# Lone-exponential step of the attention stage: VectorE copies one transposed half out of PSUM, minimum and reciprocals stand later

## Chip, cores and metric

The kernel runs on one core of one Trainium2 chip. The metric is the device time of one execution in microseconds (us). TensorE is PE (its weight loads PEld), VectorE is DVE, ScalarE is ACT, GpSimd is POOL, and the SyncE queue is SP.

## What is computed

Bucketed attention over 4 batches, 8 heads, 768 positions and head dimension 64, followed by a mixture of 8 experts in which each token goes to one expert. Cut to what matters:

```python
mask = q_bucket[:, :, :, None] == k_bucket[:, :, None, :]       # 6 sign bits of q @ proj, k @ proj
scores = scale * np.matmul(q, k.transpose(0, 1, 3, 2))          # (4, 8, 768, 768)
scores = np.where(mask, scores, -1e9)
attn = np.exp(scores - scores.max(-1, keepdims=True))
attn = attn / (attn.sum(-1, keepdims=True) + 1e-9)
x = np.matmul(attn, v)                                          # then reshaped to (3072, 512)
e = argmax(x @ w_gate); y = relu(x @ w1[e]) @ w2[e]             # times two gates
```

## The kernel before

The attention stage works in 192 steps (`NSTEP`), each for one tile of 128 queries by 768 keys of one head. Six steps make a period (`PER`), so there are 32 periods; a pair of heads takes two of them. In the text the periods are numbered 0 to 31 and the steps of a period 0 to 5 (`k` in the code), and "the first step" is step 0, "the fourth step" is step 3, which the change touches.

Per tile, in this order:

- `scores` (L536): PE makes the tile in PSUM with four matmuls, into one of two buffers `ps_s`. VectorE reads it once (L540), writes it negated and masked to SBUF as `sc`, and has the row minimum `mn` of it as an accumulated output. This frees the `ps_s` buffer, so the scores of step s need the minimum of step s-2.
- `soft` (L548): ScalarE takes the exponential in place, with the row sum as accumulated output. One exponential stands alone in each period: that of step 1's tile, issued at the end of step 2. The other five are issued in the next period's step 0.
- `normal` (L555, L556, L558): for two tiles at a time, VectorE adds 1e-9 to the sums and takes reciprocals, and GpSimd multiplies both tiles. For the pair with the lone exponential this stands in step 3.
- `transposed` (L569, L574, L572): six steps after its scores, PE transposes the tile, three 128x128 blocks into one `ps_t` buffer (there are two) and three into the other; each half is copied to `pts` in SBUF, by ScalarE (L574), and for the last six tiles the second half by VectorE (L572). The transposes of step s need the copies of step s-1 to be done, half by half.
- `weighted` (L584): in step 0 PE multiplies the transposed tiles with the values, and VectorE copies the result out (L587).

All four compute engines run in the order in which the program is written (`manual_schedule`); the loop at the end of the attention stage writes it. Other work is hung into it by `plan` (behind the step's transposes) and `block` (at named places of step 0). What matters here:

- In step 0 of every even period from 2 to 28, the next pair of heads is prepared: GpSimd makes two high parts `xl` (`split_hi`, L494) ahead of step 0's exponentials, and VectorE makes four low parts `yl` (`split_lo`, L502) between its reciprocals; the first low part of a head needs that head's high part. GpSimd runs its multiplications of the period before ahead of `split_hi`.
- `tokens` (L628, three transposes on PE and a reduction on VectorE) stands in step 2 of periods 9, 10, 17, 18, 25, 26 and 31.
- `ranks` (L695 to L700, five small operations of VectorE) stands in step 2 of periods 11, 19 and 27; `pick` (L784 to L793, seven) in step 2 of period 28; `table` (six matmuls on PE) in step 3 of periods 13, 21 and 29; `early_turn` (four transposes on PE, a cast by ScalarE, and a subtraction by VectorE, L272) in steps 2 and 4 of period 30.
- GpSimd's small tables of constants stand in periods 3 to 6.

So of the 30 periods 2 to 31, thirteen have none of this in steps 2 and 3 and none of it just before (2 to 8, 14 to 16, 22 to 24); the text calls them plain. Periods 12 and 20 stand behind the periods with ranks.

Of the kernel before, what the change touches and what calls it, by code (L numbers as in the profile page):

```python
# [14 lines left out]
ALU = mybir.AluOpType  # L15
# [8 lines left out]
HS = S // 2  # L24
# [21 lines left out]
PER = 6  # L46
NFB = F // P
MASKED = 1.0e9
# [11 lines left out]
def lsh_attention_then_moe(  # L60
# [10 lines left out]
    nc = tc.nc  # L71
# [16 lines left out]
    def signed():  # L88

        for h, s in ((0, 1.0), (1, -1.0)):  # L90
            hs = slice(h * D, (h + 1) * D)
            c = 2 * NB * h
            nc.gpsimd.tensor_scalar(pjc[hs, c:c + NB], pj[hs, 0:NB], s, 0.0, ALU.mult, ALU.add)
            nc.gpsimd.tensor_scalar(pjc[hs, c + NB:c + 2 * NB], pj[hs, 0:NB], -s, 0.0, ALU.mult, ALU.add)
# [276 lines left out]
    with ExitStack() as actx:  # L371
# [6 lines left out]
        NSTEP = 12 * NP  # L378
# [7 lines left out]
        LAG = PER  # L386
# [91 lines left out]
        def first_low(part):  # L478

            st = pairs[0]  # L480
            xl, yl, xr, qk = st["xl"][1], st["yl"][1], st["xr"][1], st["qk"][1]
            if part == 0:
                nc.vector.tensor_tensor(xr[D:P], qk[D:P], f32(xl[D:P]), ALU.subtract)
                nc.gpsimd.tensor_scalar(xl[D:P], qk[0:D], -0.125, 0.0, ALU.mult, ALU.add)  # L484
            else:
                nc.vector.scalar_tensor_tensor(yl[0:D], qk[0:D], -0.125, f32(xl[0:D]), ALU.mult, ALU.subtract)
# [35 lines left out]
        def tile_of(s):  # L522

            g, hf, i = s // 12, (s % 12) // 6, s % 6
            t, j = (i % 3, i // 3) if s // 6 in (0, 2) else (i // 2, i % 2)
            return g, hf, 3 * hf + t, j

        def scores(s):
            g, hf, t, j = tile_of(s)
            st = pairs[g]  # L530
            qs = slice(t * P, (t + 1) * P)
            ss = ps_s.tile([P, 2, 512], F32, name="ps_s")
            kb = D + 2 * NB
            for l, r, k, first in ((st["xl"][j], st["xr"][j], P, True), (st["yl"][j], st["yr"][j], kb, False)):
                for n in range(2):
                    nc.tensor.matmul(ss[:, n, 0:HS], l[0:k, qs], r[0:k, n * HS:(n + 1) * HS],  # L536
                                     start=first, stop=not first)
            sc = tp.tile([P, 2, HS], F32, name="sc", bufs=LAG + 2)
            mn = sp.tile([P, 1], F32, name="mn", bufs=PER + 2)
            nc.vector.tensor_scalar(sc, ss[:, :, 0:HS], MASKED, None, ALU.min, ALU.min, accum_out=mn)  # L540
            return sc, mn

        def soft(s, sc, mn):
            if s % GROUP == 0:
# [12 lines left out]
            for k in range(GROUP):  # L557
                nc.gpsimd.tensor_scalar(live[s0 + k], live[s0 + k], rs[:, k:k + 1], 0.0, ALU.mult, ALU.add)  # L558

        def transposed(s, pr):  # L560
            g, hf, t, j = tile_of(s)
            hb, t = s // 6, t - 3 * hf
            if s % 6 == 0:
                blocks[hb] = [tp.tile([P, NT, HS], F32, name=f"pts{n}") for n in range(2)]
            pts = blocks[hb][j]
            for h in range(2):
                tr = ps_t.tile([P, 3, P], F32, name="ps_t")
                for c in range(3):
                    nc.tensor.transpose(tr[:, c], pr[:, (3 * h + c) * P:(3 * h + c + 1) * P], ident)  # L569
                dst = pts[:, 3 * h:3 * h + 3, t * P:(t + 1) * P]  # L570
                if h and s >= NSTEP - PER:
                    nc.vector.tensor_copy(dst, tr)  # L572
                else:
                    nc.scalar.copy(dst, tr)  # L574
# [286 lines left out]
        with tc.manual_schedule(engines=MANUAL):  # L861
# [7 lines left out]
            def turn_idle(n):  # L869
                for i in range(n):  # L870
                    nc.tensor.transpose(idle[:, i % 3], ident, ident)
# [4 lines left out]
            live = {}  # L876
# [12 lines left out]
            def normals():  # L889
                while ready:  # L890
                    normal(ready.pop(0))
# [5 lines left out]
            for s in range(NSTEP + LAG):  # L897
                k = s % PER
                if s < NSTEP:
                    live[s] = scores(s)  # L900
                    raw.append(s)
                if s < 2:
                    first_low(s)
                if s == 1:
                    signed()
                if 0 < s < 3:
                    turn_idle(6)
                if s < PER:
                    normals()
                    softs(1)  # L910
                elif k == 0:
                    now("head")
                    softs(2)
                    now("early")
                    normals()
                    now("amid")
                    softs(2)
                    normals()
                    for when in ("logits", "matmuls", "behind"):
                        now(when)  # L920
                    softs(1)
                elif k == 3:
                    normals()
                if s >= LAG:
                    transposed(s - LAG, live.pop(s - LAG))
                if s >= PER and k == 2:
                    softs(1)
                for fn in at.get(s, ()):
                    fn()
# [257 lines left out]
```

## Time and profile before

| | |
|---|---|
| median of 3 runs | 764.87 us (764.33 to 765.95) |
| profiled execution | 763.37 us, of which the trace's span is 761.6 us |
| PE busy | 744.8 us, 98% of the span |
| DVE busy | 489.1 us, 64% |
| ACT busy | 458.8 us, 60% |
| POOL busy | 378.4 us, 50% |

The attention stage takes about 444 us of the span, up to the first of the experts' products at 443.94 us. A matmul's end is modelled in this profile, so a busy PE can still be waiting: one reads PE from the start of one row to the start of the next. The same six transposes and four matmuls follow each other in every step, so a step that starts late beside its neighbours shows a wait, even where the view lists no idle time.

### The profile page before, as it was taken

To read this page: it belongs to the slowest core of one execution; us is meant where nothing else is said; L and a number is where in the kernel's file an instruction comes from. 1 tells how busy PE (TensorE), PEld (TensorE's weight loads), DVE (VectorE), ACT (ScalarE), POOL (GpSimd) and SP (SyncE) were. 2 spreads that over 40 slices of the span, in tenths; PEclk is the share of its full clock that TensorE was granted. 3 is DMA by queue.
4 is the path that set the end of the run, shared out by engine and by line. 5 is a ranking of instruction groups with operands and counts; after the bars stand their busy time and mean duration, and the time that the engine had idled before them with its cause. 6 is when DMAs were issued, how large, how long until landed. Compare 5 with 4: busy or idle time off the path is not lost. (4 is left out here: it accounts for less than half of the span.)

```text
span 761.6 us, 13702 instructions
## 1 busy us (share of the span) xinstructions
PE 744.8 (98%) x4690; PEld 606.9 (80%) x4690; DVE 489.1 (64%) x1042; ACT 458.8 (60%) x928; POOL 378.4 (50%) x418
## 2 busy tenths in 40 slices
PE   7799999999999999999999999999999999999996
PEld 5677777768777686767778678988999999989895
DVE  5767766888776798767898775346354546465540
ACT  5688887887887787787787822343333434443331
POOL 7456645544554555455456932645446364645201
PEclk9999999999999999999999999999999999999999
DMA  4565555646455556645455332463445454537501
GB/s 168 135 138 124 131 138 130 125 111 133 110 135 127 128 111 136 141 106 124 82 114 131 79 96 76 150 236 107 133 137 159 153 159 146 184 127 234 187 12 40
DMA packets 84799, 98.89 MB, mean 130 GB/s; under 512 B 57999, under 2 KB 59439, under 8 KB 84720
## 3 DMA queue, kind: packets, MB, share of 16 engines
q1 hardware_dynamic: 79376, 84.58, 43.0%
q0 software_dynamic: 5200, 13.31, 5.5%
q8 instruction: 40, 0.66, 0.4%
q14 instruction: 39, 0.32, 0.1%
q10 hardware_dynamic: 144, 0.02, 0.0%
HBM read 59.49 MB, written 13.11 MB: 95 GB/s over the span
## 5 line engine op out<-in xcount | busy, mean ns | idle before, releaser
L558 POOL TENSOR_SCALAR sc<-sc,rsum 128x768 f32<-128x768 f32 x192 | 185.8, 982 | 191.2 <-DVE rsum L556 101.3
L540 DVE TENSOR_SCALAR_CACHE_REDUCE sc<-ps_s 128x768 f32<-128x768 f32 x192 | 182.7, 955 | 56.3 <-PE ps_s L536 53.4
L574 ACT COPY pts<-ps_t 128x384 f32<-128x384 f32 x378 | 162.8, 483 | 83.8 <-PE ps_t L569 82.8
L548 ACT ACTIVATE sc<-sc,mn 128x768 f32<-128x768 f32 x192 | 178.2, 935 | 7.7 <-DVE sc L540 7.7
L569 PE MATMUL ps_t<-ident,sc 128*128 128x128 f32 x1152 | 161.0, 276 | 3.2 <-POOL sc L558 2.3
L569 PEld LDWEIGHTS ps_t<-ident,sc 128*128 128x128 f32 x1152 | 133.6, 141 | 33.1 <-POOL sc L558 15.8
L584 PE MATMUL ps_a<-pts,vt 128*64 128x384 f32 x768 | 131.1, 490 | 0.0
L536 PE MATMUL ps_s<-xr,xl 128*128 128x384 f32 x384 | 115.3, 381 | 4.4 <-POOL xl L484 2.2
L584 PEld LDWEIGHTS ps_a<-pts,vt 128*64 128x64 f32 x768 | 52.2, 137 | 67.7 <-issue 67.5
L326 DVE SCALAR_TENSOR_TENSOR hl<-ps_s,hh 128x256 fp32r<-128x256 f32 (+8 forms) x40 | 34.0, 849 | 107.8 <-ACT hh L325 107.8
L536 PE MATMUL ps_s<-yr,yl 76*128 76x384 f32 x384 | 99.7, 341 | 0.7 <-POOL yr L446 0.5
L315 PE MATMUL ps_s<-xh,w1h 128*128 128x256 f32 (+7 forms) x288 | 96.9, 336 | 0.0
L315 PE MATMUL ps_s<-xlo,w1h 128*128 128x256 f32 (+7 forms) x288 | 95.3, 331 | 0.0
L315 PE MATMUL ps_s<-xh,w1l 128*128 128x256 f32 (+7 forms) x288 | 95.1, 330 | 0.0
L289 POOL DMA_INDIRECT xq<-x_dram,idx x75 | 82.7, 1103 | 23.7 <-issue 20.8
L332 POOL DMA_INDIRECT out_dram<-yo,sid x29 | 30.8, 1062 | 115.4 <-ACT yo L331 57.0
L325 ACT ACTIVATE hh<-ps_s 128x256 fp32r<-128x256 f32 (+8 forms) x40 | 29.0, 726 | 96.0 <-PE ps_s L315 96.0
L536 PEld LDWEIGHTS ps_s<-yr,yl 76*128 76x128 f32 x384 | 70.6, 191 | 1.2 <-POOL yr L446 1.2
L536 PEld LDWEIGHTS ps_s<-xr,xl 128*128 128x128 f32 x384 | 58.5, 192 | 8.0 <-DVE sc L540 3.8
L315 PEld LDWEIGHTS ps_s<-xh,w1h 128*128 128x128 f32 x288 | 54.1, 188 | 2.0 <-issue 0.6
L315 PEld LDWEIGHTS ps_s<-xlo,w1h 128*128 128x128 f32 x288 | 54.1, 188 | 1.3 <-DVE xlo L272 0.2
L315 PEld LDWEIGHTS ps_s<-xh,w1l 128*128 128x128 f32 x288 | 54.1, 188 | 1.1
(206 smaller groups left out, 1014.3 us busy)
## 6 DMA issues: line engine op xcount, KB each, us to landing
w_raw<-in_w_dram SPq DMA_DIRECT2D x34, 512.0 KB
qk<-in_qkT_dram SPq DMA_DIRECT2D x32, 384.0 KB
xh<-in_w_dram SPq DMA_DIRECT2D x14, 512.0 KB
xlo<-in_w_dram SPq DMA_DIRECT2D x14, 512.0 KB
vt<-in_v_dram SPq DMA_DIRECT2D x16, 384.0 KB
xr<-xl SPq DMA_DIRECT2D x30, 192.0 KB
yr<-xl SPq DMA_DIRECT2D x30, 192.0 KB
xr<-yl SPq DMA_DIRECT2D x30, 192.0 KB
```

The lines of the kernel that those rows point to most:

```text
L289: nc.gpsimd.indirect_dma_start(out=xq[:, k * P:(k + 1) * P], out_offset=None, in_=x_dram.rearrange("n (a f) -> (n a) f", a=NB32), in_offse ...
L315: nc.tensor.matmul(ps, l, r, start=first and k == 0, stop=last and k == len(pairs) - 1)
L325: nc.scalar.activation(hh, ph, AF.Relu)
L326: return lambda: nc.vector.scalar_tensor_tensor(hl, ph, 0.0, f32(hh), ALU.max, ALU.subtract)
L332: nc.gpsimd.indirect_dma_start(out=out[:, :], out_offset=bass.IndirectOffsetOnAxis(ap=sid[0:n, r, a:a + 1], axis=0), in_=yo[0:n], in_offse ...
L536: nc.tensor.matmul(ss[:, n, 0:HS], l[0:k, qs], r[0:k, n * HS:(n + 1) * HS], start=first, stop=not first)
L540: nc.vector.tensor_scalar(sc, ss[:, :, 0:HS], MASKED, None, ALU.min, ALU.min, accum_out=mn)
L548: nc.scalar.activation(pr, pr, AF.Exp, bias=mn, scale=-1.0, accum_out=sums[s // GROUP][:, k:k + 1])
L558: nc.gpsimd.tensor_scalar(live[s0 + k], live[s0 + k], rs[:, k:k + 1], 0.0, ALU.mult, ALU.add)
L569: nc.tensor.transpose(tr[:, c], pr[:, (3 * h + c) * P:(3 * h + c + 1) * P], ident)
L574: nc.scalar.copy(dst, tr)
L584: nc.tensor.matmul(st["av"][j * D:(j + 1) * D], st["v"][:, j, c], blocks[hb][j][:, c], start=(c == 0), stop=(c == NT - 1))
```

## The change

In periods 2 to 31, in step 3 alone:

- VectorE, not ScalarE, copies the first half of the transposed tile out of PSUM (L572 in place of L574); ScalarE keeps the second half.
- That step's minimum (L540) is issued behind this copy, no longer right behind the step's matmuls.
- The addition and reciprocal for the pair with the lone exponential, and GpSimd's two multiplications that need them, are issued in step 4, behind that step's minimum, no longer in step 3.

```diff
@@ scores @@
-            nc.vector.tensor_scalar(sc, ss[:, :, 0:HS], MASKED, None, ALU.min, ALU.min, accum_out=mn)
-            return sc, mn
+            return (sc, mn), lambda: nc.vector.tensor_scalar(sc, ss[:, :, 0:HS], MASKED, None, ALU.min, ALU.min,
+                                                             accum_out=mn)
@@ transposed @@
-        def transposed(s, pr):
+        def transposed(s, pr, behind=False):
...
-                if h and s >= NSTEP - PER:
+                if h and s >= NSTEP - PER or behind and not h:
                     nc.vector.tensor_copy(dst, tr)
                 else:
                     nc.scalar.copy(dst, tr)
@@ the loop over steps @@
-                    live[s] = scores(s)
+                    live[s], least = scores(s)
                     raw.append(s)
+                    if s < 2 * PER or k != 3:
+                        least()
...
-                elif k == 3:
+                elif k == 4 or k == 3 and s < 2 * PER:
                     normals()
                 if s >= LAG:
-                    transposed(s - LAG, live.pop(s - LAG))
+                    transposed(s - LAG, live.pop(s - LAG), 2 * PER <= s < NSTEP and k == 3)
+                    if 2 * PER <= s < NSTEP and k == 3:
+                        least()
```

VectorE's order in a plain period before, from the last work of step 0 on. The first three minimums are those of steps 1 to 3, the next three those of steps 4, 5 and 0:

```order
L596 STREAM_TRANSPOSE xb<-ot 128x384
L540 TENSOR_SCALAR sc,mn<-ps_s 128x768 x3
L555 TENSOR_SCALAR rsum<-rsum 128x2
L556 RECIPROCAL rsum<-rsum 128x2
L540 TENSOR_SCALAR sc,mn<-ps_s 128x768 x3
L502 SCALAR_TENSOR_TENSOR yl<-qk,pj,xl 128x384
```

The reciprocals for the pair with the lone exponential stand between the third and the fourth of these six. The same place in the changed kernel, where the two minimums behind the copy are those of steps 3 and 4:

```order
L596 STREAM_TRANSPOSE xb<-ot 128x384
L540 TENSOR_SCALAR sc,mn<-ps_s 128x768 x2
L572 COPY pts_680<-ps_t 128x3x128
L540 TENSOR_SCALAR sc,mn<-ps_s 128x768 x2
L555 TENSOR_SCALAR rsum<-rsum 128x2
L556 RECIPROCAL rsum<-rsum 128x2
L540 TENSOR_SCALAR sc,mn<-ps_s 128x768 x2
L502 SCALAR_TENSOR_TENSOR yl<-qk,pj,xl 128x384
```

The copy L572 has come in between the minimums of steps 2 and 3, and the pair L555, L556 has gone from behind step 3's minimum to behind step 4's.

VectorE's order in a period with ranks, in the changed kernel (`off`, `rank`, `tot` and `base` are the ranks' tiles):

```order
L540 TENSOR_SCALAR sc,mn<-ps_s 128x768 x2
L695 TENSOR_TENSOR off<-ps_m,base 128x48
L696 TENSOR_TENSOR off<-off,oneh 128x48
L697 TENSOR_REDUCE rank<-off 128x6
L699 TENSOR_REDUCE tot<-ps_m 128x8
L700 TENSOR_TENSOR base<-base,tot 128x8
L572 COPY pts_2122<-ps_t 128x3x128
L540 TENSOR_SCALAR sc,mn<-ps_s 128x768 x2
```

Here the copy stands behind the five operations that were planned into step 2, which stood between the minimums of steps 2 and 3 before as well. On GpSimd the order stays, but for one place in period 30, where a weight's split, planned into step 3, now stands ahead of the two multiplications.

## Rows read from the trace of the kernel before

**Rows 1.** Timeline of a plain period (tile numbers 132 to 137 are scored from 299.15 us on): start in us, duration in us, engine, line, operation, output<-inputs, shapes, number of merged instructions, and in brackets the idle time of the engine before it and its releaser. From the third step's transposes to the end of the period, PE with the ACT, DVE and POOL rows between.

```profile
306.82 0.82 PE L569 MATMUL ps_t<-ident,sc 128*128 128x128 f32 x6
...
308.10 0.95 ACT L548 ACTIVATE sc<-sc,mn 128x768 f32<-128x768 f32 x1
308.18 0.82 PE L569 MATMUL ps_t<-ident,sc 128*128 128x128 f32 x6
...
308.38 0.96 DVE L540 TENSOR_SCALAR_CACHE_REDUCE sc<-ps_s 128x768 f32<-128x768 f32 x1 [0.40 <-PE ps_s L536]
...
309.03 0.85 ACT L574 COPY pts<-ps_t 128x384 f32<-128x384 f32 x2
...
309.65 0.84 PE L569 MATMUL ps_t<-ident,sc 128*128 128x128 f32 x6
309.80 1.79 POOL L558 TENSOR_SCALAR sc<-sc,rsum 128x768 f32<-128x768 f32 x2 [2.97 <-PE ps_s L536]
...
310.25 0.59 PE L536 MATMUL ps_s<-xr,xl 128*128 128x384 f32 x2
...
311.04 0.82 PE L569 MATMUL ps_t<-ident,sc 128*128 128x128 f32 x6
...
311.57 0.86 ACT L574 COPY pts<-ps_t 128x384 f32<-128x384 f32 x2 [0.51 <-PE ps_t L569]
```

**Rows 2.** Timeline of the last tiles' transposes, where VectorE already evicts second halves (same columns).

```profile
440.62 0.56 DVE L572 COPY pts<-ps_t 128x384 f32<-128x384 f32 x1 [0.64 <-PE ps_t L569]
```

**Rows 3.** Timeline of the period in which the first expert is picked, fourth and fifth step: VectorE's last small operation of `pick`, the minimum behind it, and PE (same columns).

```profile
388.24 0.82 PE L569 MATMUL ps_t<-ident,sc 128*128 128x128 f32 x6
...
389.30 0.16 DVE L793 SCALAR_TENSOR_TENSOR base<-lead,base 128x8 f32<-128x8 f32 x1
389.38 0.95 DVE L540 TENSOR_SCALAR_CACHE_REDUCE sc<-ps_s 128x768 f32<-128x768 f32 x1
...
389.61 0.82 PE L569 MATMUL ps_t<-ident,sc 128*128 128x128 f32 x6
...
390.39 0.62 PE L536 MATMUL ps_s<-xr,xl 128*128 128x384 f32 x2
...
391.21 0.82 PE L569 MATMUL ps_t<-ident,sc 128*128 128x128 f32 x6
```

**Rows 4.** Timeline of a period with three extra transposes on PE in its third step (the logits' tokens): PE from the fourth step's transposes to the sixth step's (same columns).

```profile
348.25 0.82 PE L569 MATMUL ps_t<-ident,sc 128*128 128x128 f32 x6
...
350.18 0.59 PE L536 MATMUL ps_s<-xr,xl 128*128 128x384 f32 x2
...
350.96 0.82 PE L569 MATMUL ps_t<-ident,sc 128*128 128x128 f32 x6
```

**Rows 5.** Timeline of a period in which VectorE makes the ranks in the third step: PE's fourth-step transposes, VectorE's last operation of `ranks`, and PE's scores of the sixth step (same columns).

```profile
161.98 0.82 PE L569 MATMUL ps_t<-ident,sc 128*128 128x128 f32 x6
...
162.63 0.17 DVE L700 TENSOR_TENSOR base<-base,tot 128x8 f32<-128x8 f32 x1
...
164.05 0.60 PE L536 MATMUL ps_s<-xr,xl 128*128 128x384 f32 x2
```

**Rows 6.** Timeline of the period of the early gather's transposes: VectorE's subtraction for them and PE's fifth-step transposes (same columns).

```profile
415.95 0.69 DVE L272 TENSOR_TENSOR xlo<-ps_m,xh 128x512 fp32r<-128x512 f32 x1 [1.06 <-ACT xh L271]
...
416.44 0.84 PE L569 MATMUL ps_t<-ident,sc 128*128 128x128 f32 x6
```

**Rows 7.** Timeline of the first steps of a period whose first step prepares the next pair of heads: GpSimd's two high parts, VectorE's low parts (L502), sums (L555), output copy (L587) and second step's minimum, PE's scores of the fourth step (same columns).

```profile
324.93 1.79 POOL L494 TENSOR_SCALAR xl<-qk,pj 128x768 fp32r<-128x768 f32 x2
...
326.82 0.61 DVE L502 SCALAR_TENSOR_TENSOR yl<-qk,pj,xl 128x384 fp32r<-128x384 f32 x1
...
329.39 0.30 DVE L555 TENSOR_SCALAR rsum<-rsum 128x2 f32<-128x2 f32 x1 [0.42 <-ACT sc L548]
...
329.88 0.56 DVE L587 COPY ot<-ps_a 128x384 f32<-128x384 f32 x1
...
330.35 0.61 DVE L502 SCALAR_TENSOR_TENSOR yl<-qk,pj,xl 128x384 fp32r<-128x384 f32 x1
...
331.38 0.96 DVE L540 TENSOR_SCALAR_CACHE_REDUCE sc<-ps_s 128x768 f32<-128x768 f32 x1
...
333.12 0.60 PE L536 MATMUL ps_s<-xr,xl 128*128 128x384 f32 x2
```

**Rows 8.** Timeline near the start of the kernel, where a low part on VectorE starts while a high part runs on GpSimd (same columns).

```profile
16.79 1.78 POOL L494 TENSOR_SCALAR xl<-qk,pj 128x768 fp32r<-128x768 f32 x2
...
17.72 1.25 DVE L502 SCALAR_TENSOR_TENSOR yl<-qk,pj,xl 128x384 fp32r<-128x384 f32 x1 [1.76 <-POOL xl L494]
```

**Rows 9.** Timeline of the first step of another period that prepares a pair: two low parts merged, and the sum behind them (same columns).

```profile
302.12 1.77 DVE L502 SCALAR_TENSOR_TENSOR yl<-qk,pj,xl 128x384 fp32r<-128x384 f32 x2
...
303.81 0.16 DVE L555 TENSOR_SCALAR rsum<-rsum 128x2 f32<-128x2 f32 x1
```

**Rows 10.** Timeline of GpSimd from the end of period 3 to the high parts of period 4, with a table of constants left out between (same columns).

```profile
58.16 1.79 POOL L558 TENSOR_SCALAR sc<-sc,rsum 128x768 f32<-128x768 f32 x2 [3.18 <-ACT pts L574]
...
60.28 1.79 POOL L494 TENSOR_SCALAR xl<-qk,pj 128x768 fp32r<-128x768 f32 x2
```

**Rows 11.** Timeline of the period behind the one with ranks: the second step's minimum on VectorE and the fourth step's scores on PE (same columns).

```profile
172.86 0.91 DVE L540 TENSOR_SCALAR_CACHE_REDUCE sc<-ps_s 128x768 f32<-128x768 f32 x1
...
173.84 0.62 PE L536 MATMUL ps_s<-xr,xl 128*128 128x384 f32 x2
```

## The prediction

> **What bounds the kernel now.** I read the page first: PE is busy almost all of the span, so I then read PE's starts in the timeline of the attention stage, and last who stands next to each late start. In a plain period [rows 1] the transposes of the third and fourth step start 1.36 us apart (306.82, 308.18), which is PE's own pace. From the fourth to the fifth step it is 1.47 (309.65), and to the sixth 1.39 (311.04). So PE loses 0.11 + 0.03 = 0.14 us in such a period. The cause stands between: the lone exponential on ACT starts at 308.10 and takes 0.95, so ACT's two copies of the fourth step's tile start only at 309.03, although the copies of the sixth step start 0.53 behind their transposes (311.04 to 311.57). The fifth step's transposes want the buffers that these copies free. Where PE has three more transposes in the third step, the exponential is through in time, and nothing is lost: 2.71 us from the fourth step's transposes to the sixth's (348.25 to 350.96) [rows 4], against 2.86 in the plain period.
>
> **What the change buys.** ACT's first copy of the fourth step goes, its second one starts right behind the exponential, and DVE frees the first buffer. The 0.14 us lie on the path, since PE sets the end, and they are what can be won: there are 13 plain periods, and 3 with ranks that show the same 2.07 us to the sixth step's scores (161.98 to 164.05) [rows 5]: 16 x 0.14 = 2.2 us. ACT's 0.43 us themselves are off the path.
>
> **What it adds on DVE, and who waits for that.** The copy now stands ahead of the fourth step's minimum, and behind that minimum are queued the fifth step's minimum, the reciprocals and all later work of DVE. PE's scores of the sixth step need the fourth step's minimum for their PSUM buffer. I count from the start of the fourth step's transposes:
>
> - the copy starts at 0.53, as ACT's would [rows 1]; it takes 0.56 [rows 2];
> - the next operation of DVE starts 0.47 behind the start of such a copy (329.88 to 330.35) [rows 7], so the minimum starts at 1.00 in place of 0.20 (308.38);
> - where PE already waits for such a minimum, its scores start 1.01 behind the minimum's start (389.38 to 390.39) [rows 3], so they start at 2.01 or a little later, and the transposes behind them 0.82 later (391.21): 2.83 to 2.84.
>
> That is against 2.86 today in a plain period and 2.71 where nothing waits. **The wait does not go, it changes hands.** In 13 plain periods the gain is 0.02 each: -0.3. In the 7 periods with tokens in the third step, and in 12 and 20, where PE's wait ahead of the fourth step [rows 11] gives ACT its time, it costs 0.13 each: 9 x 0.13 = +1.2. In the 3 periods with a table in the fourth step PE has so much work there that nothing shows: 0.
>
> [...]
>
> **Where DVE is already late.** With ranks, DVE's last small operation ends 0.82 behind the transposes (162.63 + 0.17) [rows 5], the next may start 0.08 earlier (as 389.38 against 389.30 + 0.16 [rows 3]), so the copy starts at 0.74, the minimum at 1.21, the scores at 2.22 in place of 2.07, and with 0.03 for the longer step behind a wait that is 0.19 each: 3 x 0.19 = +0.6. With `pick`, the copy takes the minimum's place at 1.14 (388.24 to 389.38) [rows 3], and the scores start 0.47 later: +0.5. In period 30 the copy must wait for the subtraction that ends at 416.64 [rows 6]; it ends near 417.1, and only then may the fifth step's transposes start, which start at 416.44 today: +0.7, with the scores behind them.
>
> **What the moved reciprocals do.** GpSimd's two multiplications start 1.62 behind the fourth step's transposes today (309.80). In the change they come behind the fifth step's minimum, which starts 0.88 behind the fourth's, so at 1.88; from that minimum to the multiplications it takes what it takes today from 308.38 to 309.80, 1.42; so they start at 3.3, 1.6 to 1.7 us later. The tiles are transposed a period later, so PE does not feel this. But GpSimd's next work in an even period are the two high parts (324.93, 1.79 for both) [rows 7], and the first low part on DVE (326.82) needs the first of them. Today it ends about a microsecond early; in the change the low part starts some 0.7 later, and then beside the second high part. A low part that starts beside one takes 1.25 [rows 8], not 0.61 [rows 7]. So DVE is about 1.2 us late at the sums behind it, allowing for the 0.1 that it waits there today. How much reaches PE? In one kind of period the sums wait 0.42 for ACT today (329.39), which absorbs that much; in the other kind they wait for nothing (the low parts end at 303.89, the sum starts at 303.81) [rows 9]. The chain ends with the second step's minimum, which must start 1.01 before the fourth step's scores: at 331.38 it has 333.12 - 331.38 - 1.01 = 0.73 to spare. So PE waits 1.2 - 0.73 = 0.47 in periods 8, 14 and 22, and about nothing in 16 and 24; in 4 and 6 GpSimd's constants stand in between as well (0.33, from 58.16 + 1.79 to 60.28) [rows 10], so some 0.4 there: 1.4 + 0.8 = +2.2. The bounds are 0, if the late low parts pair up better, and 7 x 1.1 = 7.7, if the last low part collides with a multiplication too (0.64 more each). I take 2.2, nearest to the rows. Periods 10, 18 and 26 have more work on PE ahead of their fourth step: 0. In 12, 20 and 28 PE already waits for the second step's minimum (172.86 to 173.84) [rows 11], and DVE comes out of the period with ranks 0.47 - 0.19 = 0.28 later beside PE: 3 x 0.28 = +0.8.
>
> **The sum.** -0.3 + 1.2 + 0.6 + 0.5 + 0.7 + 0.8 + 2.2 = +5.7 us. No later stage gives it back: PE is the busy engine behind attention too, and the experts start with what attention yields. Against the profiled execution that is 763.37 + 5.7 = 769.1; the median of the runs lies 1.5 higher, so 770.6, of which I write 770.5.
>
> **Rivals.**
>
> *The wait at the fifth step goes and none comes* (faster). [...] As a mechanism here: the minimum behind the copy would have to start by 0.9, so that the scores start at 1.93 as in [rows 4]; then the 2.2 us are won: 762.7. For it speaks that DVE is busy only two thirds of the time; against it, that DVE's three steps are each read from a row, and that 0.1 us would have to vanish from them. From the point where the copy and its release cost 0.37 instead of 0.47 it decides. Chance 0.07.
>
> *Hands change and little else happens* (no difference). The plain periods gain 0.05 each, the copy runs 0.05 faster on the path, and the delay at the start of the even periods is absorbed whole: -0.7 + 0.7 + 0.5 + 0.4 + 0.6 + 0 = +1.5 or less, so 764 to 766.4. For it: the margin of 0.73 and the 0.42 of slack are read, the collision is one row; against it: two terms must come out well at once. Chance 0.15.
>
> *The moved multiplications collide twice* (slower still). The last low part (330.35) starts beside a multiplication in all seven periods: 7 x 0.64 = 4.5 more, 775. Chance 0.13.
>
> **How the numbers follow.** A run of this kernel can tell about 0.2%, or 1.5 us, from no change. The forecast, slower by 2 to 8 us, has 0.65; with the third rival the chance of slower is 0.78, of the same 0.15, of faster 0.07. The range that leaves two in ten out goes from 766.0, where the even periods absorb everything, to 774.0, where half of the collisions happen.
>
> **What would show it.** In the changed profile a plain period's transposes start 1.36 apart from the fourth to the fifth step, and about 1.47 from the fifth to the sixth, with DVE's minimum ending just before the sixth step's scores. In periods with tokens the latter is 1.47 as well. In even periods the first low part is 1.25 long, and in some the third to fourth step is above 1.36. It is wrong if the sixth step's scores start at 1.93, if the first low part is 0.61 long, or if PE's starts slip at a place not named here.

## The result: 771.71 us, slower by 1%

| | before | changed |
|---|---|---|
| median of 6 runs each | 764.19 us (763.35 to 765.95) | 771.71 us (770.49 to 773.69) |
| ratio to before, 95% interval | | 1.0096 (1.0079 to 1.0112) |
| profiled execution, its span | 763.37 us, 761.6 us | 773.69 us, 772.0 us |
| PE busy | 744.8 us, 98% | 751.4 us, 97% |
| DVE busy | 489.1 us, 64% | 504.4 us, 65% |
| ACT busy | 458.8 us, 60% | 449.5 us, 58% |

The time lies in the forecast's range, 1.2 us above the forecast. ACT has lost its 30 copies (348 of L574 are left of 378) and DVE has won them, as written. The medians differ by 7.5 us, the spans by 10.4, since the profiled execution of the changed kernel is the slowest of its six. I therefore read the attention stage by itself: from the first step's scores of one period to those of the next, on PE, in both traces (period 31 to the transposes that follow it). Over periods 2 to 31 the differences add up to 7.83 us. Of the other 2.6 us, 1.2 lie ahead of period 2, which the change leaves as it was (there the granted clock from 18 to 36 us is 0.81 in this execution and 0.89 in the other), and 1.4 behind attention, where PE stands 1.22 us with no releaser at 506.33 us. In the traces of the eight experiments the same two stretches lie between 1.4 us below and 1.3 above, and between 0.6 below and 1.7 above the kernel before, whatever was edited; so I count neither to the change.

**A plain period**, the timeline that answers to [rows 1], from the fourth step's transposes on:

```profile
313.81 0.82 PE L569 MATMUL ps_t<-ident,sc 128*128 128x128 f32 x6
...
314.34 0.56 DVE L572 COPY pts<-ps_t 128x384 f32<-128x384 f32 x1 [0.53 <-PE ps_t L569]
...
314.67 0.48 ACT L574 COPY pts<-ps_t 128x384 f32<-128x384 f32 x1 [0.15 <-PE ps_t L569]
314.82 0.95 DVE L540 TENSOR_SCALAR_CACHE_REDUCE sc<-ps_s 128x768 f32<-128x768 f32 x1
...
315.17 0.82 PE L569 MATMUL ps_t<-ident,sc 128*128 128x128 f32 x6
...
315.83 0.62 PE L536 MATMUL ps_s<-xr,xl 128*128 128x384 f32 x2
...
316.65 0.82 PE L569 MATMUL ps_t<-ident,sc 128*128 128x128 f32 x6
...
317.10 1.79 POOL L558 TENSOR_SCALAR sc<-sc,rsum 128x768 f32<-128x768 f32 x2 [3.84 <-DVE rsum L556]
...
317.22 0.60 PE L536 MATMUL ps_s<-xr,xl 128*128 128x384 f32 x2
```

The fifth step's transposes now start 1.36 behind the fourth's (313.81 to 315.17), where it was 1.47. The sixth's start 1.48 behind those (to 316.65), where it was 1.39. One wait is gone and the other has come, and PE has 2.84 us in place of 2.86. The chain is the one that was drawn: copy 0.53 behind the transposes, minimum 0.48 behind the copy, scores 1.01 behind the minimum (314.82 to 315.83). GpSimd's multiplications stand 3.29 behind the transposes in place of 1.62. No idle time of PE is listed here; only the distance of the starts shows the wait.

**An even period** (24), the timeline that answers to [rows 7]:

```profile
332.13 1.79 POOL L494 TENSOR_SCALAR xl<-qk,pj 128x768 fp32r<-128x768 f32 x2
...
333.07 1.25 DVE L502 SCALAR_TENSOR_TENSOR yl<-qk,pj,xl 128x384 fp32r<-128x384 f32 x1 [0.59 <-POOL xl L494]
...
334.76 4.54 POOL L558 TENSOR_SCALAR sc<-sc,rsum 128x768 f32<-128x768 f32 x4 [0.85 <-DVE rsum L556]
...
335.56 0.81 DVE L555 TENSOR_SCALAR rsum<-rsum 128x2 f32<-128x2 f32 x1
...
338.05 0.91 DVE L540 TENSOR_SCALAR_CACHE_REDUCE sc<-ps_s 128x768 f32<-128x768 f32 x1
...
339.03 0.62 PE L536 MATMUL ps_s<-xr,xl 128*128 128x384 f32 x2
```

The first low part now runs beside the second high part and takes 1.25 in place of 0.61, as foreseen; the text calls it a collision when an operation of VectorE lasts longer beside one of GpSimd. The second pair's sum, L555 at 335.56, takes 0.81 in place of 0.30, which was not foreseen. Counted from PE's products of the first step (325.74 before, 331.31 now), the second step's minimum starts 6.74 in place of 5.64 behind them, 1.10 late against 0.73 to spare, and the fourth step's scores are 0.34 late.

**The periods 10, 18 and 26** lose 0.44 each at the sixth step's transposes, a place that the prediction does not name. The timeline of period 26 before, from the fifth step's transposes to the sixth's (L646 and L648 are two operations of the routing function `best`, planned into the fourth step; `df` is the difference to the row's largest logit):

```profile
363.03 0.82 PE L569 MATMUL ps_t<-ident,sc 128*128 128x128 f32 x6
...
363.26 0.21 DVE L646 TENSOR_TENSOR df<-lgt,mx 128x48 f32<-128x48 f32 x1
...
363.50 0.24 ACT L648 ACTIVATE ex<-df 128x48 f32<-128x48 f32 x1 [0.43 <-DVE df L646]
...
363.78 0.84 ACT L574 COPY pts<-ps_t 128x384 f32<-128x384 f32 x2
...
364.39 0.85 PE L569 MATMUL ps_t<-ident,sc 128*128 128x128 f32 x6
```

The same place in the changed kernel, from the fourth step's minimum on:

```profile
368.72 0.95 DVE L540 TENSOR_SCALAR_CACHE_REDUCE sc<-ps_s 128x768 f32<-128x768 f32 x1
...
369.08 0.82 PE L569 MATMUL ps_t<-ident,sc 128*128 128x128 f32 x6
...
369.59 0.20 DVE L644 TENSOR_REDUCE mx<-lgt 128x6 f32<-128x48 f32 x1
...
369.82 0.21 DVE L646 TENSOR_TENSOR df<-lgt,mx 128x48 f32<-128x48 f32 x1
...
370.07 0.24 ACT L648 ACTIVATE ex<-df 128x48 f32<-128x48 f32 x1 [1.02 <-DVE df L646]
...
370.35 0.84 ACT L574 COPY pts<-ps_t 128x384 f32<-128x384 f32 x2
...
370.95 0.85 PE L569 MATMUL ps_t<-ident,sc 128*128 128x128 f32 x6 [0.26 <-ACT pts L574]
```

ACT's small exponential stands ahead of its two copies of the fifth step and wants `df`. VectorE makes `df` behind the minimum that the change made late. Before, the exponential starts 0.47 behind the fifth step's transposes and the copies 0.75 behind them. Now it is 0.99 and 1.27, ACT stands idle for 1.02 ahead of it, and the sixth step's transposes start 1.87 behind the fifth's in place of 1.36: the 0.08 at the scores that every period with tokens pays, and 0.44.

**Period 30** loses 1.09 at its third step's transposes, which the prediction does not name either. GpSimd and PE before (L257 is the early gather's indirect DMA, L178 and L181 split a weight; the first row is the pair with the lone exponential of period 29, the second the first of two gathers):

```profile
402.77 1.79 POOL L558 TENSOR_SCALAR sc<-sc,rsum 128x768 f32<-128x768 f32 x2 [3.04 <-DVE rsum L556]
...
405.86 1.18 POOL L257 DMA_INDIRECT xg<-x_dram,gid  x1 [1.30 <-DVE gid L803]
...
409.48 2.38 POOL L181 TENSOR_TENSOR w1l<-w_raw,w1h 128x1024 fp32r<-128x1024 f32 x1
...
411.83 2.68 POOL L558 TENSOR_SCALAR sc<-sc,rsum 128x768 f32<-128x768 f32 x3
...
413.13 0.82 PE L569 MATMUL ps_t<-ident,sc 128*128 128x128 f32 x6
```

And in the changed kernel:

```profile
412.58 1.84 POOL L558 TENSOR_SCALAR sc<-sc,rsum 128x768 f32<-128x768 f32 x2 [5.52 <-DVE tacc_e L232]
...
414.60 1.18 POOL L257 DMA_INDIRECT xg<-x_dram,gid  x1 [0.17 <-DVE sc L540]
...
417.08 1.06 POOL L178 TENSOR_SCALAR w1h<-w_raw 128x1024 fp32r<-128x1024 f32 x1
...
418.22 2.39 POOL L181 TENSOR_TENSOR w1l<-w_raw,w1h 128x1024 fp32r<-128x1024 f32 x1
...
420.59 2.67 POOL L558 TENSOR_SCALAR sc<-sc,rsum 128x768 f32<-128x768 f32 x3
...
421.55 0.88 PE L569 MATMUL ps_t<-ident,sc 128*128 128x128 f32 x6 [0.93 <-POOL sc L558]
```

The order on GpSimd is the same in both kernels up to here, and both splits last as long as before. But the two multiplications of period 29 come later. Their reciprocals stand behind the fifth step's minimum now, and in period 29, which has a table in its fourth step, that step is late on PE as well: counted from the fourth step's transposes of period 29 (400.82 and 408.15), they start at 4.43 in place of 1.95. The 1.30 us in which GpSimd stood idle ahead of the gather are gone (0.17 are left), and the gather starts at 6.44 in place of 5.04. So the splits end 1.4 later, and the third step's tile gets its multiplication 1.49 behind the second step's transposes (419.10 to 420.59) in place of 0.06 (411.77 to 411.83). Before, the first of the three multiplied tiles was ready (411.83 and some 0.9) 0.4 ahead of its transposes; now they wait for it, 0.93 by the bracket and 1.09 by the starts.

### The profile page after: what moved, and what is told of

It is laid out like the page before. It is cut to its first block, busy times and chain, and to the rows that moved or that the text cites. A ratio compares the mean times of both kernels' runs of the same rounds, so it can differ in the third digit from the quotient of the medians.

```text
span 772.0 us, 13685 instructions
## 1 busy us (share of the span) xinstructions
PE 751.4 (97%) x4690; PEld 610.6 (79%) x4690; DVE 504.4 (65%) x1072; ACT 449.5 (58%) x898; POOL 380.5 (49%) x418
## 5 line engine op out<-in xcount | busy, mean ns | idle before, releaser
L574 ACT COPY pts<-ps_t 128x384 f32<-128x384 f32 x348 | 151.7, 482 | 99.8 <-PE ps_t L569 98.9
L540 DVE TENSOR_SCALAR_CACHE_REDUCE sc<-ps_s 128x768 f32<-128x768 f32 x192 | 179.8, 951 | 32.6 <-PE ps_s L536 31.1
L569 PEld LDWEIGHTS ps_t<-ident,sc 128*128 128x128 f32 x1152 | 135.3, 141 | 33.5 <-issue 15.6
```

What stands on the lines that cost most here:

```text
L540: return (sc, mn), lambda: nc.vector.tensor_scalar(sc, ss[:, :, 0:HS], MASKED, None, ALU.min, ALU.min, accum_out=mn)
```

## The experiments

Each ratio is to the kernel before on the same chip, in one group of runs (medians of before 762.82, 763.05 and 764.66 us in the three groups); "the trace" is the sum over periods 2 to 31 as above, against the profiled execution of before.

### The copy alone, and the reciprocals alone

The change with the addition, the reciprocal and the multiplications back in the fourth step, behind that step's late minimum:

```diff
-                elif k == 4 or k == 3 and s < 2 * PER:
+                elif k == 3 and not 2 * PER <= s < NSTEP:
                     normals()
...
                     if 2 * PER <= s < NSTEP and k == 3:
                         least()
+                        normals()
```

> The copy and the minimum behind it as in the change, but the addition, the reciprocal and GpSimd's multiplications back in the fourth step, behind that step's minimum. My theory (the change loses in two ways: PE waits for the late minimum, and GpSimd's moved multiplications hold up the high parts in even periods and the gather's queue in period 30): the multiplications start some 0.8 us later than before instead of 1.6, so the even periods' waits at the fourth step go (about 3 us) and most of the 1.1 us in the third step of period 30; the logits' maximum comes still later on VectorE in periods 10, 18 and 26 (about 1 us more in all). In total +4 to +5 us over the kernel before, against +7.5 for the change. Rival (the copy ahead of the minimum is the whole cost, the reciprocals' place does not matter): +7 to +8 us.

Measured: 768.19 against 762.82 us, ratio 1.0067 (1.0052 to 1.0082); the trace gives +4.95, as expected. The waits of the even periods are gone (-0.02 to -0.04 in each), and so is period 30's third step (+0.47 left of 1.61). Periods 10, 18 and 26 get worse, 0.71 at the sixth step, since the two small operations of the reciprocal stand ahead of `df` as well. In 12, 20 and 28 the fourth step's scores lose 0.27, 0.33 and 0.27.

The kernel before with nothing but the later reciprocals and multiplications:

```diff
-                elif k == 3:
+                elif k == 4 or k == 3 and s < 2 * PER:
                     normals()
```

> The kernel before, with only the addition, the reciprocal and the multiplications moved into the fifth step; ScalarE copies both halves and the minimum stays where it was. My theory: no wait for the minimum at the sixth step, the 0.14 us at the fifth step stay; the waits at the fourth step of even periods come, a little smaller (the multiplications are 1.4 instead of 1.6 us late), and the one of about 1 us in period 30: +2.5 to +4 us over the kernel before. Rival (only the copy costs): within 1 us of the kernel before.

Measured: 764.65 against 762.82 us, ratio 1.0026 (1.0014 to 1.0037), +1.1 to +2.8 us; the trace gives +1.78, less than the 2.5 to 4 that were expected. Of it, 1.13 are period 30, whose third step waits 0.92 for GpSimd as in the change. The even periods wait 0.35 and 0.31 in 4 and 6, 0.21 and 0.23 in 14 and 22, and 0.00 to 0.07 in 8, 16 and 24, and get 0.11 of that back at the fifth step.

So each half of the change costs by itself, and the copy costs most. 4.95 + 1.78 = 6.73, and the change has 7.83: the even periods wait 2.78 with both parts and 1.24 with the reciprocals alone, since with both the high parts start some 0.3 later still in five of the seven; periods 10, 18 and 26 pay less with both, since the reciprocals no longer stand ahead of `df`.

### The high parts out of the way

The change, with GpSimd's high parts planned three steps earlier, into the fourth step of the period ahead, from the third pair on:

```diff
-                block(s0, "head", *(lambda g=g, j=j: split_hi(g, j) for j in range(2)))
+                highs = [lambda g=g, j=j: split_hi(g, j) for j in range(2)]
+                plan(s0 - 3, *highs) if g > 2 else block(s0, "head", *highs)
```

> The change, with GpSimd's two high parts for the next pair issued in the fourth step of the period before (from the third pair on), ahead of the moved multiplications. My theory: the first low part no longer starts late nor beside a high part, so the waits at the fourth step of the even periods go (3.4 us by the trace, some 0.3 of it perhaps left behind the periods with ranks): +4 to +5 us over the kernel before. Rival (those waits come from VectorE's own lag behind the copy, not from GpSimd's queue): +7 to +8 us, fourth step as in the change.

Measured: 768.90 against 762.82 us, ratio 1.0081 (1.0065 to 1.0096); the trace gives +5.61, above the 4 to 5 that were expected. All seven plain even periods from 4 on lose their wait (-0.02 to -0.04). So their 2.78 us hung on the high parts behind the late multiplications. The rest is not all kept: period 11 waits 0.30 at its second step's scores, and at the fourth step's 12 waits 0.51 in place of 0.16 and 28 0.55 in place of 0.15, while 20 gains 0.2. In period 12 the high parts now stand beside VectorE's last small operations of the period with ranks (L201, L204; start, duration and the rest as above):

```profile
165.99 0.91 POOL L494 TENSOR_SCALAR xl<-qk,pj 128x768 fp32r<-128x768 f32 x1 [0.76 <-PE ps_s L536]
...
166.31 0.63 DVE L201 TENSOR_TENSOR t_ge<-rank,chki 128x30 f32<-128x30 f32 x1
...
166.88 1.80 POOL L558 TENSOR_SCALAR sc<-sc,rsum 128x768 f32<-128x768 f32 x2
...
166.97 0.85 DVE L204 TENSOR_TENSOR t_oa<-t_ge 128x24 f32<-128x24 f32 x1
```

They take 0.63 and 0.85, where the changed kernel has 0.17 and 0.18 for the same two, so VectorE's minimums and low parts behind them come late. So the high parts moved from one collision into another.

### `best` a step later

```diff
-                          (15, r["best"]), (18, r["prefix"]), (20, r["ranks"]), (22, r["places"]),
+                          (16, r["best"]), (18, r["prefix"]), (20, r["ranks"]), (22, r["places"]),
```

> The change, with the logits' maximum and its two exponentials (best) planned one step later, into the fifth step of periods 10, 18 and 26, so that they stand behind the copies of that step on ScalarE. My theory: the 0.44 us ahead of the sixth step's transposes in these three periods come from ScalarE, which waits for the late maximum ahead of its copies; they go, -1.3 us against the change: +5.5 to +6.5 us over the kernel before, and the sixth step's transposes in these periods start 0.8 behind its scores. Rival (the 0.44 come from VectorE's lag at the sixth step itself): as the change, +7 to +8.

Measured: 771.65 against 762.82 us, ratio 1.0119 (1.0102 to 1.0137); the trace gives +7.62, below that interval (its own execution, 769.64 us, was the fastest of the four), so I read from it only the places. The place is right: the sixth step's transposes lose their 0.44 in 10, 18 and 26. The saving that was expected is not there: the next period's second-step scores wait 0.40 more (0.39 to 0.40 in 11, 19 and 27). Period 27 of this kernel, PE, ACT and DVE:

```profile
368.71 0.84 ACT L574 COPY pts<-ps_t 128x384 f32<-128x384 f32 x2
...
369.21 4.09 PE L584 MATMUL ps_a<-pts,vt 128*64 128x384 f32 x24
...
369.44 0.94 ACT L548 ACTIVATE sc<-sc,mn 128x768 f32<-128x768 f32 x1
...
374.91 0.67 DVE L417 TENSOR_SCALAR bt<-ps_m,pj 128x384 fp32r<-128x384 f32 x1
...
375.63 0.18 PE L685 MATMUL ps_m<-ohb,tri 128*128 128x48 bf16 x1 [0.74 <-DVE bt L417]
```

ACT's two small exponentials now delay the sixth step's copies, and with them the period's first large exponential: it starts 0.23 behind PE's products (369.21 to 369.44), where the changed kernel has it 0.19 ahead (372.25 to 372.44). The whole chain of the first step hangs on it, and PE waits 0.74 for `bt` in place of 0.34. In the changed kernel ACT has no gap for this pair of exponentials at either of the two steps.

### Where nothing else is hit

The copy and the late minimum in the 13 plain periods only, reciprocals in the fourth step:

```diff
+PLAIN = (2, 3, 4, 5, 6, 7, 8, 14, 15, 16, 22, 23, 24)
...
-                    if s < 2 * PER or k != 3:
+                    if s // PER not in PLAIN or k != 3:
                         least()
...
-                elif k == 4 or k == 3 and s < 2 * PER:
+                elif k == 3 and not s // PER in PLAIN:
                     normals()
                 if s >= LAG:
-                    transposed(s - LAG, live.pop(s - LAG), 2 * PER <= s < NSTEP and k == 3)
-                    if 2 * PER <= s < NSTEP and k == 3:
+                    transposed(s - LAG, live.pop(s - LAG), s // PER in PLAIN and k == 3)
+                    if s // PER in PLAIN and k == 3:
                         least()
+                        normals()
```

> VectorE's copy and the minimum behind it in the 13 plain periods alone (2 to 8, 14 to 16, 22 to 24), with the reciprocals kept in the fourth step; all other periods as before. My theory (in a plain period the wait at the fifth step only turns into one of nearly the same length at the sixth): 0.03 to 0.05 us won in each, -0.4 to -0.6 us over the kernel before in all, which the timing can hardly tell from none. [...]

Measured: 762.42 against 763.05 us, ratio 0.9993 (0.9981 to 1.0004); the trace gives -0.38. Each plain period gains 0.11 at the fifth step's transposes, loses 0.05 at the sixth step's scores, and ends 0.02 to 0.04 shorter. The full 0.14 in each, a gain of 1.8 us or more (ratio below 0.9976), lies outside the interval: in the very place for which the copy was moved, the wait changes hands.

The same kernel with the copy made twice, a second one of the same data:

```diff
+                if behind and not h:
+                    nc.vector.tensor_copy(dst, tr)
                 if h and s >= NSTEP - PER or behind and not h:
```

> As f1_plain_only, with VectorE's copy made twice in a row (same data, the second copy is waste). My theory: the minimum starts 0.48 us later once more, and all of it reaches the sixth step's scores, so each of the 13 plain periods is 0.44 us longer than before: +5 to +6.5 us over the kernel before; the fifth step's transposes start some 0.26 late as well, inside that. Rival (PE's sixth step waits for something other than this minimum): within 1 us of f1_plain_only, or only the 0.26 at the fifth step.

Measured: 770.60 against 763.05 us, ratio 1.0098 (1.0082 to 1.0115); the trace gives +7.28, +0.56 or +0.57 in each of the 13 periods and at most 0.07 in any other. That is above the 5 to 6.5 that were expected. VectorE and PE in period 22 of this kernel:

```profile
314.92 0.56 DVE L573 COPY pts<-ps_t 128x384 f32<-128x384 f32 x1 [0.72 <-PE ps_t L570]
...
315.51 0.56 DVE L575 COPY pts<-ps_t 128x384 f32<-128x384 f32 x1
...
315.98 0.95 DVE L541 TENSOR_SCALAR_CACHE_REDUCE sc<-ps_s 128x768 f32<-128x768 f32 x1
...
316.99 0.62 PE L537 MATMUL ps_s<-xr,xl 128*128 128x384 f32 x2 [0.28 <-DVE sc L541]
```

The minimum starts 1.06 behind the first copy in place of 0.48, since the second copy starts 0.59 behind the first, and the scores start 1.01 behind the minimum, as ever. Beside the kernel with one copy each of these periods is 0.58 to 0.61 longer: all of VectorE's added 0.58 reaches PE, so VectorE has no slack at all at this place, though it is busy for 64% of the span in the kernel before and 65% in the changed one.

### The exponential in two halves

The rival way to the same wait: the kernel before, VectorE's order untouched, the lone exponential in two halves of 384 columns, one at the end of the second step and one at the end of the third, in all periods from 2 to 29 except 12, 20 and 28. VectorE adds the two row sums (one more small operation).

```diff
+            if half is not None:
+                cols = slice(half * HS, (half + 1) * HS)
+                pr = sc.rearrange("p a b -> p (a b)")
+                if half == 0:
+                    rest[s] = sp.tile([P, 1], F32, name="rest")
+                nc.scalar.activation(pr[:, cols], pr[:, cols], AF.Exp, bias=mn, scale=-1.0,
+                                     accum_out=rest[s] if half else sums[s // GROUP][:, 1:2])
+                return pr
...
+            if s0 + 1 in rest:
+                nc.vector.tensor_tensor(rs[:, 1:2], rs[:, 1:2], rest.pop(s0 + 1), ALU.add)
...
-                if s >= PER and k == 2:
+                if k in (1, 2) and s // PER in HALVES:
+                    lone = raw[0] if k == 1 else raw.pop(0)
+                    if k == 1:
+                        kept = live[lone]
+                        soft(lone, *kept, half=0)
+                    else:
+                        live[lone] = soft(lone, *kept, half=1)
+                        ready.append(lone - 1)
+                elif s >= PER and k == 2:
                     softs(1)
```

> The kernel before, with the lone exponential cut into two halves of 384 columns, one at the end of the second step and one at the end of the third (each with its own sum, and one small addition on VectorE), in periods 2 to 29 but for 12, 20 and 28; copies, minimums and multiplications stay where they were. Each half should take some 0.6 us, which fits between ScalarE's copies without holding the buffers. My theory (the 0.14 us come from ScalarE's copies behind the whole exponential, and VectorE need not be touched to win them): 16 x 0.14 = -2.2 us, with what two instructions cost extra -1.5 to -2.3 us, ratio 0.997 to 0.998. Rival (the 0.14 are PE's own, or ScalarE's extra fixed cost eats them): within 1 us, or slower.

Measured: 762.77 against 763.05 us, ratio 0.9998 (0.9987 to 1.0009); the trace gives -0.04, where 1.5 to 2.3 less was expected. The 13 plain periods and the three with ranks gain 0.12 to 0.14 each, 2.1 in all. The 0.26 to 0.27 at the sixth step of 10, 18 and 26 (`df` again, behind the added operation of VectorE), 0.39, 0.46 and 0.32 at the fourth step's scores of 12, 20 and 28, and 0.13 in 29 take 2.1 back. Ahead of period 12, VectorE is 0.4 late from the added operation on, and still 0.39 late at the second step's minimum, for which PE waits there; why 29 loses is not shown.

With the halves in the 13 plain periods alone:

```diff
-HALVES = tuple(m for m in range(2, 30) if m not in (12, 20, 28))
+HALVES = (2, 3, 4, 5, 6, 7, 8, 14, 15, 16, 22, 23, 24)
```

> As f3_exponential_halves, in the 13 plain periods alone, so that neither the logits' maximum (10, 18, 26) nor the periods behind the ranks (12, 20, 28) see VectorE's small addition. My theory: 13 x 0.13 = -1.7 us by the trace's periods 2 to 31, and a ratio near 0.998. Rival (the gain of f3's plain periods is taken back elsewhere whatever the others do): the trace's sum within 0.3 us of none.

Measured: 761.92 against 764.66 us, ratio 0.9966 (0.9952 to 0.9979), 1.6 to 3.7 us faster; the trace gives -1.82, -0.13 or -0.14 in each of the 13 periods. Period 22 of this kernel, from the third step's transposes on:

```profile
305.86 0.63 ACT L551 ACTIVATE sc<-sc,mn 128x384 f32<-128x384 f32 x1
305.94 0.82 PE L581 MATMUL ps_t<-ident,sc 128*128 128x128 f32 x6
...
307.21 0.63 ACT L551 ACTIVATE sc<-sc,mn 128x384 f32<-128x384 f32 x1
307.30 0.82 PE L581 MATMUL ps_t<-ident,sc 128*128 128x128 f32 x6
...
307.83 0.86 ACT L586 COPY pts<-ps_t 128x384 f32<-128x384 f32 x2
...
308.66 0.82 PE L581 MATMUL ps_t<-ident,sc 128*128 128x128 f32 x6
...
310.02 0.82 PE L581 MATMUL ps_t<-ident,sc 128*128 128x128 f32 x6
```

A half takes 0.63 and not 0.95, so ACT's copies of the fourth step start 0.53 behind their transposes (307.30 to 307.83) in place of 0.85 [rows 1], and every step of PE is 1.36 again. This version beats both kernels. So here two halves won 0.13 or 0.14 us in each of the 13 periods, with ACT busy for 60% of the span in the kernel before, and nobody waits in them for the engine that adds up the pieces; with the halves in 25 periods the waits of others took the gain back (ratio 0.9998).

## Why the prediction came out as it did

| term | predicted, us | measured, us |
|---|---|---|
| plain periods, 13 | -0.3 | -0.2 |
| periods with tokens, 12 and 20 (9) | +1.2 | +0.9 |
| ranks (3) | +0.6 | +0.5 |
| `pick`, period 28 | +0.5 | +0.4 |
| period 30, behind the subtraction | +0.7 | +0.5 |
| even periods, fourth step's scores (7) | +2.2 | +2.8 |
| 12, 20 and 28, fourth step's scores | +0.8 | +0.4 |
| table, periods 13, 21, 29 | 0 | 0.0 |
| 10, 18 and 26, sixth step's transposes | not named | +1.3 |
| period 30, third step's transposes | not named | +1.1 |
| sum | +5.7 | +7.8 |

**The wait changes hands: right, and shown.** The three steps of the chain measured 0.53, 0.48 and 1.01 where 0.53, 0.47 and 1.01 were read from [rows 1, 3, 7]. The copy in the plain periods alone brings at most 1.5 us (interval), and the second copy passes to PE whole. The first rival, in which the wait at the fifth step goes and none comes, is not borne out: the ratio is 0.9993 (0.9981 to 1.0004) with the copy in the very periods that should gain. Both kernels read PSUM with both engines already, and the engine to which the copy goes also reads the other PSUM buffer that PE wants.

**Ranks, `pick`, tokens and the subtraction of period 30: right**, each within 0.3 us for the group. In period 30 the copy ends 2.14 behind the fourth step's transposes, where the prediction has it. But only the second three of the fifth step's transposes wait for it (425.64, 0.20 with L572 as the releaser); the first three start at 1.48, as before. So it costs 0.5 and not 0.7.

**Even periods: the mechanism right, one slack misread.** Taking the high parts out of the way removes the whole wait, and the first low part took its 1.25. But the prediction let 16 and 24 go free, since "in one kind of period the sums wait 0.42 for ACT today (329.39), which absorbs that much". They lost 0.27 and 0.34. That 0.42 was no slack. In the trace's single records the sum L555 ends 0.02 behind the first of GpSimd's multiplications before (329.66 and 329.68) and 0.03 behind it now (336.34 and 336.37). By these ends it is the multiplication that sets when the sum is done, and that starts 0.33 behind the reciprocal ahead of it (327.76 to 328.09, 334.44 to 334.76); the wait for ACT only lay in front of an end that was fixed anyway. This is read from the rows and was not tested by a run of its own.

The reciprocal is 1.10 later, and so is the sum's end, although the sum starts only 0.60 later and then lasts 0.81. In the other kind of period it comes to the same: in period 14 the third low part collides and takes 1.26 before and the sum 0.16, while now it takes 0.61 and the sum 0.80. All these periods are 1.0 to 1.1 late against the 0.73 to spare, in place of 1.2 in some and 0.8 in others: 0.22 to 0.35 in 8, 14, 16, 22 and 24. In 4 and 6, where GpSimd's constants stand in between, it was 0.71 and 0.67 in place of 0.4. The rival that let the last low part collide as well did not come: that part takes at most 0.70 in place of 0.61 [rows 7].

In 12, 20 and 28 the prediction had VectorE come 0.28 late each time. PE waits 0.12 to 0.16 longer there, and not for that reason: VectorE comes early, and loses it again. In period 28 the small operations L204 and L208 took 0.85 and 0.74 before, beside a multiplication and a high part that are now later, and take 0.18 and 0.69. VectorE's first minimum behind them starts 0.6 earlier (0.75 behind the period's first scores in place of 1.36), and the first low part then gives 0.64 of it back.

**Not followed: two queues.** The prediction said that "behind that minimum are queued the fifth step's minimum, the reciprocals and all later work of DVE", but followed only those that PE waits for directly. `df` of `best` is among that later work; ACT waits for it with two copies queued behind, and PE waits for these: +1.3. And "the tiles are transposed a period later, so PE does not feel this" is true of the two moved multiplications and not of what they push back on GpSimd in period 30: gather, weight split, and then a multiplication that PE wants in the same period: +1.1. The prediction has neither of the slacks on the way, 1.30 ahead of the gather and 0.4 ahead of the transposes at 413.13. (The new order on GpSimd that the section on the change names in period 30 concerns a later split and is not the cause.) That the reciprocals alone bring 1.08 of it, and the copy alone none, shows whose it is; that the copy alone makes the `df` wait larger (0.71), and that `best` a step later removes it, shows the other.

So the forecast's direction and its first mechanism held, the terms that were named came to 5.4 of 5.7, and the missing 2.4 us are the two places that were not named. Such a slip of PE is one of the prediction's own signs of being wrong, and there it was wrong. That the time came within 1.2 us of the forecast is in part luck. The even periods cost 0.6 more than their term and the other terms 0.9 less; and the medians differ by 7.5 in place of 5.7 us, but the median before was 764.19 over six runs and not 764.87. The lower end of the range does not follow from its reason either: without the 2.2 of the even periods the sum is still 3.5, and the time 768.3 in place of 766.0.

## What to carry to other kernels

An eviction given to a second engine is worth only what that engine has free at that point of its order, not over the span (here 0.02 to 0.04 us a plain period, on an engine busy for 64% of it): read, from start to start, who waits for the instruction that it is put ahead of. When a shared instruction is made later, follow every engine that waits for anything behind it, and then what stands behind that engine's wait, until each branch ends in a slack that a row shows. Here the better cut was at the instruction that blocks: half an exponential earlier cost its own engine some 0.3 us a period (two halves of 0.63 in place of 0.95) and won the whole wait (0.13 or 0.14 us), once it was kept out of the periods in which a neighbour had no room.

## What the runs showed that was not expected

- An operation of VectorE on two numbers per partition (L555) took up to 0.81 us where it started within a multiplication of GpSimd, and 0.15 to 0.17 where it was free; where it was long, it ended 0.02 to 0.03 behind the multiplication. At five places in the kernel before (one is the sum of [rows 9]) it took 0.15 to 0.16 although the record of a multiplication had begun; that multiplication itself had begun beside a low part and lasted 1.20 or 1.21 in place of 0.91. Why the long ones wait is not shown. GpSimd takes longer as well: a multiplication that starts within VectorE's pair of low parts lasted 1.57 before and 1.58 now in the single records of period 24, in place of the 0.90 or 0.91 of one alone.
- VectorE's copy of 384 elements out of PSUM delays the next, different operation by 0.48 but a second such copy by 0.59 (314.92 to 315.51). The second copy has the same source and the same destination; no run shows whether that makes the difference.
- A half of the exponential costs 0.63 and the whole 0.95, so two halves cost ACT 1.26. If the cost is linear in the size, an estimate from these two is that 0.31 us of each are there whatever the size.
